# Sliding-window attention and soft-MoE slots: mask by a TensorE product, weight loads in quarter pieces in a fixed order

## The chip, the cores and the metric

The kernel runs on one core of one Trainium2 chip. The metric is the device time of one execution in microseconds, as the median of several runs; one further execution is profiled. PE is the matrix engine (TensorE), PEld its weight loads, DVE VectorE, ACT ScalarE, POOL GpSimd, SP the engine that issues the output transfers.

## The reference

Causal sliding-window attention (window 64) over q, k, v of 8 batches, 8 heads, 576 positions, 64 values per head; its output, as x of 4608 rows by 512, goes through a soft mixture of 8 experts with 4 slots each.

```python
scores = scale * np.matmul(q, k.transpose(0, 1, 3, 2))
rel = pos[:, None] - pos[None, :]
mask = (rel >= 0) & (rel < window)
scores = np.where(mask, scores, -1000000000.0)
attn = softmax(scores, -1)
x = (attn @ v) laid out as (B * S, H * D)

logits = x @ phi                                  # (4608, 32)
d = softmax(logits, 0); slot_input = d.T @ x      # 32 slots
slot_out[e] = np.maximum(slot_input[e] @ w1[e], 0.0) @ w2[e]   # e = 0..7
return softmax(logits, 1) @ slot_out
```

Inputs and output are 32-bit floats; w1[e] is 512 x 1024, w2[e] 1024 x 512.

## The kernel before

The attention runs over 16 units; a unit is one half (four heads) of one batch. Its q, k and v are loaded by three transfers issued on Pool's queue (`load_unit`, line 56), which also turn them into 16-bit floats, 288 KB each in SBUF; three buffers of each kind rotate. A weight tile, w1 or w2 of one expert, is one transfer of 1024 KB on the same queue (`load_w1`, `load_w2`, lines 70 and 74); the w2 of the last expert goes in two transfers into a buffer that held attention output. Eight w1 and seven w2 buffers mean that no other weight load waits for a buffer.

Work on unit u is cut into three steps j (eight windows of 64 queries in steps 0 and 1, one window per head pair in step 2). In each step the loop of lines 316 to 332 emits:

- `stage_t2(u, j)` (line 160): PE transposes of v (line 167) into a PSUM tile `tr`, and two copies on VectorE into `vw` (line 169);
- `stage_s(u, j)` (line 173): score matmuls (line 182) into the PSUM tile `sc`, the two halves x of the heads lying on partitions 0 to 63 and 64 to 127 and in two banks; Exp on ScalarE into `pm` (line 187); then the mask, two products on VectorE (line 191) with the 0/1 tile `mask0`;
- `stage_t1(u + 1, j)` (line 147): PE transposes of the next unit's q (j = 0), k (j = 1) or v (j = 2) (line 136) in two `tr` tiles, copied to SBUF by ScalarE for q and v (line 143), by VectorE for k (line 141);
- `stage_av` of the step before (line 198): the attention product (line 214) and the division on VectorE (lines 220 to 231); line 229 writes the last chunk of a unit;
- one piece of the MoE work of a finished batch (`stage_xt` to `stage_et`, lines 241 to 294), each with a `tr`-tagged PSUM tile.

`tr` has two PSUM buffers, `sc` two, `av` one. After unit 15 come the rest of the MoE work, `dinv` and `slot_inT` (lines 351 and 352), then the experts (`hp` line 362, `sop` line 382) and the output stage (`cp` line 398, `ob` lines 402 and 404, output transfers from SP).

The program is written with a tile framework. The order on each engine is not that of the source: a scheduler takes, among the instructions that it holds ready, the one of the highest priority (source order), and so a transfer that waits for no buffer can go ahead of one that does. `issue_loads` (line 303) hands it one unit's loads and one weight tile per unit:

```python
def issue_loads(u):
    if u + 2 < nu:
        load_unit(u + 2)
    for _ in range(1 if u >= 1 else 0):
        if w_order and len(w_order) > 3:
            f, e = w_order.pop(0)
            f(e)
```

Of the kernel before, what the change touches and what calls it, by code (L numbers as in the profile page):

```python
# [9 lines left out]
FP16 = mybir.dt.float16  # L10
AF = mybir.ActivationFunctionType
ALU = mybir.AluOpType
# [4 lines left out]
def kernel(  # L17
# [10 lines left out]
    nc = tc.nc  # L28

    B, H, S, Dh = q.shape  # L30
    D, NSLOT = moe_phi.shape
    E, _, F = moe_w1.shape
# [4 lines left out]
    NHD = D // 128  # L37
    NFC = F // 128
# [15 lines left out]
    loaded = {}  # L54
# [12 lines left out]

    w1_t, w2_t = {}, {}

    def load_w1(e):  # L70
        w1_t[e] = pw1.tile([128, NHD, F], FP16, name="w1s", tag="w1s")
        nc.gpsimd.dma_start(out=w1_t[e], in_=moe_w1[e].rearrange("(c p) f -> p c f", p=128))

    def load_w2(e):
        src = moe_w2[e].rearrange("(c p) d -> p c d", p=128)
        if e < E - 1:
            w2_t[e] = pw2.tile([128, NFC, D], FP16, name="w2s", tag="w2s")
            nc.gpsimd.dma_start(out=w2_t[e], in_=src)
        else:
            w2_t[e] = pxb.tile([128, NFC, D], FP16, name="w2l", tag="x_bp")  # L80
            for c in range(0, NFC, 4):
                nc.gpsimd.dma_start(out=w2_t[e][:, c:c + 4], in_=src[:, c:c + 4])

    load_unit(0)

# [2 lines left out]
    make_identity(nc, ident)  # L88
    ones = const.tile([128, 128], FP16, name="ones")
    nc.vector.memset(ones, 1.0)  # L90
    mask0 = const.tile([128, 64], FP16, name="mask0")
    nc.gpsimd.memset(mask0, 1.0)
    nc.gpsimd.affine_select(
        out=mask0, in_=mask0, compare_op=ALU.is_ge, fill=0.0,
        base=-1, pattern=[[-1, 64]], channel_multiplier=1,
    )
    nc.gpsimd.affine_select(
        out=mask0, in_=mask0, compare_op=ALU.is_ge, fill=0.0,
        base=64, pattern=[[1, 64]], channel_multiplier=-1,
    )  # L100
    kTs, vTs, vws, hTs = [], [], [], []
    for n in range(2):
        kt = const.tile([128, 2, 64 + S], FP16, name=f"kT{n}")
# [20 lines left out]
        hTs.append(ht)  # L124

    psum1 = ExitStack()
    ps = psum1.enter_context(tc.tile_pool(name="ps", bufs=2, space=bass.MemoryType.PSUM))


    def t1(src, dst, on_vector):  # L130

        for t0, n in ((0, 5), (5, 4)):
            tr = ps.tile([128, 8, 128], FP16, name="tr", tag="tr")
            for j in range(n):
                for x in range(2):
                    nc.tensor.transpose(tr[64 * x:64 * x + 64, j, :],  # L136
                                        src[:, x, 64 * (t0 + j):64 * (t0 + j) + 64], ident[:, :])
            o = dst.rearrange("p h (g t) -> p h g t", t=T)[:, :, :, t0:t0 + n]
            i = tr[:, 0:n, :].rearrange("p t (h g) -> p h g t", h=2)
            if on_vector:  # L140
                nc.vector.tensor_copy(out=o, in_=i)  # L141
            else:
                nc.scalar.copy(out=o, in_=i)  # L143

    state = {}

    def stage_t1(u, which):
        if which == 0:
            qT = pqt.tile([128, 2, S], FP16, name="qT", tag="qT")
            state[u] = dict(qT=qT, kT=kTs[u % 2], vT=vTs[u % 2], vw=vws[u % 2])  # L150
            t1(loaded[u][0], qT, False)
        elif which == 1:
            t1(loaded[u][1], state[u]["kT"][:, :, 64:64 + S], True)
        else:
            t1(loaded[u][2], state[u]["vT"][:, :, 64:64 + S], False)

    def steps(j):
        return range(4 * j, 4 * j + 4) if j < 2 else range(8, 9)
# [1 line left out]
    def stage_t2(u, j):  # L160
        st = state[u]
        wins = list(steps(j))
        n = len(wins)
        tr = ps.tile([128, 8, 128], FP16, name="tr", tag="tr")
        for h in range(2):
            for w, i in enumerate(wins):
                nc.tensor.transpose(tr[:, h * n + w, :], st["vT"][:, h, 64 * i:64 * i + 128], ident[:, :])  # L167
        for h in range(2):
            nc.vector.tensor_copy(  # L169
                out=st["vw"][:, wins[0]:wins[0] + n, h::2, 0:64],  # L170
                in_=tr[:, h * n:h * n + n, :].rearrange("p w (x d) -> p w x d", x=2))

    def stage_s(u, j):
        st = state[u]
        wins = list(steps(j))
        n = len(wins)
        sc = ps.tile([128, 2, 512], FP32, name="sc", tag="sc")
        for h in range(2):
            for w, i in enumerate(wins):
                for x in range(2):  # L180
                    o = 64 * (h * n + w)
                    nc.tensor.matmul(sc[:, x, o:o + 64],
                                     st["kT"][64 * x:64 * x + 64, h, 64 * i:64 * i + 128],
                                     st["qT"][64 * x:64 * x + 64, h, 64 * i:64 * i + 64],
                                     start=True, stop=True)
        pm = ppm.tile([128, 2, 8, 64], FP16, name="pm", tag="pm")
        nc.scalar.activation(pm[:, :, 0:2 * n, :],  # L187
                             sc[:, :, 0:128 * n].rearrange("p x (w q) -> p x w q", q=64),
                             AF.Exp, scale=scale)
        for x in range(2):  # L190
            nc.vector.tensor_tensor(  # L191
                out=pm[:, x, 0:2 * n, :], in0=pm[:, x, 0:2 * n, :],
                in1=mask0[:, :].unsqueeze(1).broadcast_to([128, 2 * n, 64]), op=ALU.mult)
        st["pm", j] = pm

    xbp = {}
# [1 line left out]
    def stage_av(u, j):  # L198
        b, half = units[u]
        st = state[u]  # L200
        bp, odd = divmod(b, 2)
        if bp not in xbp:
            xbp[bp] = pxb.tile([128, 9, D], FP16, name="x_bp", tag="x_bp")
        xb = xbp[bp]
        wins = list(steps(j))
        n = len(wins)
        pm = st["pm", j]
        av = ps.tile([128, 4, 256], FP32, name="av", tag="av", bufs=1)
        for x in range(2):
            for h in range(2):  # L210
                kk = 2 * x + h
                for w, i in enumerate(wins):
                    r0 = 64 * (i % 2) if j < 2 else 64 * odd
                    nc.tensor.matmul(av[r0:r0 + 64, kk, 65 * (w // 2):65 * (w // 2) + 65],  # L214
                                     pm[:, x, h * n + w, :], st["vw"][:, i, kk, 0:65],
                                     start=True, stop=True)
        rc = psm.tile([128, 4, 2], FP32, name="rc", tag="rc")
        if j < 2:
            avv = av[:, :, 0:130].rearrange("p k (c e) -> p k c e", e=65)
            nc.vector.reciprocal(rc[:, :, :], avv[:, :, :, 64])  # L220
            c0 = 4 * odd + 2 * j
            nc.vector.tensor_tensor(  # L222
                out=xb[:, c0:c0 + 2, 256 * half:256 * half + 256].rearrange("p c (k d) -> p k c d", d=64),
                in0=avv[:, :, :, 0:64],
                in1=rc[:, :, :].unsqueeze(3).broadcast_to([128, 4, 2, 64]), op=ALU.mult)
        else:
            r = slice(64 * odd, 64 * odd + 64)
            nc.vector.reciprocal(rc[r, :, 0], av[r, :, 64])
            nc.vector.tensor_tensor(  # L229
                out=xb[r, 8, 256 * half:256 * half + 256].rearrange("p (k d) -> p k d", d=64),  # L230
                in0=av[r, :, 0:64],
                in1=rc[r, :, 0].unsqueeze(2).broadcast_to([64, 4, 64]), op=ALU.mult)
# [62 lines left out]


    nu = len(units)
    w_order = []
    for e in range(E):
        w_order += [(load_w1, e), (load_w2, e)]  # L300
    w_at = {u: 1 for u in range(3, nu)}

    def issue_loads(u):
        if u + 2 < nu:
            load_unit(u + 2)
        for _ in range(1 if u >= 1 else 0):
            if w_order and len(w_order) > 3:
                f, e = w_order.pop(0)
                f(e)

    load_unit(1)
    todo = []
# [2 lines left out]
    pend = None  # L315
    for u in range(nu):
        issue_loads(u)
        for j in range(3):
            stage_t2(u, j)
            stage_s(u, j)  # L320
            if u + 1 < nu:
                stage_t1(u + 1, j)
            if pend is not None:
                stage_av(*pend)
                pu, pj = pend
                if pj == 2 and units[pu][1] == 1:
                    b = units[pu][0]
                    todo += [lambda b=b: stage_xt(b, 0), lambda b=b: stage_xt(b, 1), lambda b=b: stage_xt(b, 2),
                             lambda b=b: stage_logit(b), lambda b=b: stage_slot(b), lambda b=b: stage_et(b)]
            pend = (u, j)  # L330
            if todo:
                todo.pop(0)()
    while w_order:
        f, e = w_order.pop(0)
        f(e)
    stage_av(*pend)
    while todo:
        todo.pop(0)()
# [106 lines left out]
```

## Time and profile before

| | us |
|---|---|
| median of 3 runs (lowest, highest) | 244.25 (244.11, 244.54) |
| the profiled execution | 244.91 |
| its span, first to last instruction | 243.0 |
| PE busy | 168.3 (69%) |
| PEld busy | 121.0 (50%) |
| DVE busy | 147.1 (61%) |
| ACT busy | 100.9 (42%) |
| POOL busy | 51.7 (21%) |

Pool's loads, the software queue, move 30.97 MB as written to SBUF; the outputs, on a hardware queue, 9.44 MB. The busy shares are means over stages that differ: attention, experts, output. The page cuts the span into 40 slices with the busy share of each engine, the granted PE clock (PEclk) and the DMA rate; other views give the instructions in order of time, stretches with busy times, groups of like instructions with their mean duration, and the chain of work that ended last. Busy time of PE includes modelled ends of pipelined matmuls.

### The profile page before, as it was taken

Reading aid. Unit: us, or ns where it says so; the run is one execution under the profiler, and the core shown is the slowest. Engines: PE = TensorE matmul, PEld = TensorE weight load, DVE = VectorE, ACT = ScalarE, POOL = GpSimd, SP = SyncE. Lnnn points to the kernel's source line nnn. Section 1 sums busy time; section 2 is a strip of 40 time slices with the busy share of each in tenths; the row PEclk is TensorE's granted clock in tenths of the full one; section 3 lists DMA queues with packets and bytes.
Section 4 is the critical chain, followed back from the end, with each engine's and each line's share of the span. In section 5 each row is a group of like instructions: output and inputs, shape, how many; then the busy total and the mean of one; then the engine's idle time right before and its main releaser. Section 6 shows DMA issues by size and latency. Waiting matters only on the chain. (4 is left out here: it accounts for less than half of the span.)

```text
span 243.0 us, 6919 instructions
## 1 busy us (share of the span) xinstructions
PE 168.3 (69%) x3028; PEld 121.0 (50%) x3028; DVE 147.1 (61%) x420; ACT 100.9 (42%) x160; POOL 51.7 (21%) x77
## 2 busy tenths in 40 slices
PE   0687677878862858749388699777866899878000
PEld 0466566667651746538266577666655444321000
DVE  1258898898882663917457486998996212199100
ACT  2456547537540705325071437367340211199000
POOL 8953342222322123231122321002000000000000
PEclk9999999999996555965756657999996599965555
DMA  5999999999999999999999999006500000079996
GB/s 86 159 192 211 206 207 210 208 209 211 208 212 205 209 208 208 211 206 211 207 209 208 207 206 163 2 3 94 84 3 0 3 0 4 0 270 378 379 374 154
DMA packets 31069, 40.83 MB, mean 168 GB/s; under 512 B 1856, under 2 KB 22336, under 8 KB 31040
## 3 DMA queue, kind: packets, MB, share of 16 engines
q0 software_dynamic: 26144, 30.97, 74.8%
q1 hardware_dynamic: 4896, 9.44, 11.3%
q8 instruction: 23, 0.38, 0.6%
q14 instruction: 6, 0.05, 0.1%
HBM read 61.93 MB, written 9.44 MB: 294 GB/s over the span
## 5 line engine op out<-in xcount | busy, mean ns | idle before, releaser
L187 ACT ACTIVATE pm<-sc 128x1024 f16<-128x1024 f32 (+1 forms) x48 | 39.1, 814 | 25.0 <-issue 18.9
L191 DVE TENSOR_TENSOR pm<-pm,mask_98 128x512 f16<-128x512 f16 (+1 forms) x96 | 30.0, 352 | 1.6 <-ACT pm L187 1.1
L136 PE MATMUL tr<-ident,vn 128*64 128x128 f16 x288 | 17.3, 258 | 19.7 <-DMA vn<-in_v_dram 17.6
L143 ACT COPY qT<-tr 128x640 f16<-128x640 f16 (+1 forms) x32 | 23.4, 746 | 10.5 <-PE tr L136 10.4
L143 ACT COPY vT_112<-tr 128x640 f16<-128x640 f16 (+1 forms) x16 | 11.8, 739 | 32.3 <-PE tr L136 32.1
L214 PEld LDWEIGHTS <-pm 128*64 128x64 f16 x576 | 21.5, 126 | 5.8 <-DVE x_bp L229 2.2
L136 PEld LDWEIGHTS <-vn 128*64 128x64 f16 x288 | 12.7, 131 | 21.2 <-DMA vn<-in_v_dram 18.8
L143 ACT COPY vT_103<-tr 128x640 f16<-128x640 f16 (+1 forms) x16 | 11.7, 739 | 27.0 <-PE tr L136 25.5
L220 DVE RECIPROCAL rc<-av 128x8 f32<-128x8 f32 x32 | 6.4, 199 | 27.2 <-PE av L214 27.2
L222 DVE TENSOR_TENSOR x_bp<-av,rc 128x512 f16<-128x512 f32 x32 | 22.0, 686 | 0.4
L136 PE MATMUL tr<-ident,qn 128*64 128x128 f16 x288 | 17.1, 263 | 6.8 <-DMA qn<-in_q_dram 5.6
L169 DVE COPY vw_104<-tr 128x512 f16<-128x512 f16 (+1 forms) x48 | 14.9, 351 | 9.4 <-PE tr L167 9.4
L136 PE MATMUL tr<-ident,kn 128*64 128x128 f16 x288 | 15.6, 249 | 5.6 <-DMA kn<-in_k_dram 2.6
L61 POOL DMA_DIRECT2D vn<-in_v_dram x16 | 11.4, 715 | 33.0 <-DMA w2s<-in_moe_w_dram 8.4
L167 PE MATMUL tr<-ident,vT_112 128*128 128x128 f16 x144 | 14.7, 251 | 5.2 <-ACT vT_112 L143 2.6
L169 DVE COPY vw_113<-tr 128x512 f16<-128x512 f16 (+1 forms) x48 | 15.1, 349 | 4.9 <-PE tr L167 4.9
L167 PE MATMUL tr<-ident,vT_103 128*128 128x128 f16 x144 | 15.2, 250 | 3.7 <-ACT vT_103 L143 1.5
L249 PE MATMUL tr<-ident,x_bp 128*128 128x128 f16 x144 | 13.3, 240 | 5.5 <-DVE kT_111 L141 2.7
L136 PEld LDWEIGHTS <-qn 128*64 128x64 f16 x288 | 11.8, 132 | 10.1 <-DMA qn<-in_q_dram 5.6
L141 DVE COPY kT_102<-tr 128x640 f16<-128x640 f16 (+1 forms) x16 | 11.7, 768 | 7.6 <-PE tr L136 7.4
L61 POOL DMA_DIRECT2D kn<-in_k_dram x16 | 11.4, 714 | 21.1 <-PE tr L136 6.9
L214 PE MATMUL av<-vw_113,pm 128*64 128x65 f16 x288 | 14.3, 216 | 1.3 <-DVE x_bp L229 0.8
(78 smaller groups left out, 284.7 us busy)
## 6 DMA issues: line engine op xcount, KB each, us to landing
out_dram<-ob SPq DMA_DIRECT2D x18, 512.0 KB, 5.5
w1s<-in_moe_w_dram POOLq DMA_DIRECT2D x8, 1024.0 KB, 25.1
w2s<-in_moe_w_dram POOLq DMA_DIRECT2D x7, 1024.0 KB, 22.1
qn<-in_q_dram POOLq DMA_DIRECT2D x16, 288.0 KB, 17.4
kn<-in_k_dram POOLq DMA_DIRECT2D x16, 288.0 KB, 15.3
vn<-in_v_dram POOLq DMA_DIRECT2D x16, 288.0 KB, 16.3
w2l<-in_moe_w_dram POOLq DMA_DIRECT2D x2, 512.0 KB, 8.6
phi_sb<-in_moe_phi_dram POOLq DMA_DIRECT2D x1, 32.0 KB, 6.4
```

The costliest lines, as they stand in the source:

```text
L61: nc.gpsimd.dma_start(out=t, in_=src[b, 4 * half:4 * half + 4].rearrange("(x h) (g t) d -> (h g) x (t d)", x=2, h=2, t=T))
L136: nc.tensor.transpose(tr[64 * x:64 * x + 64, j, :], src[:, x, 64 * (t0 + j):64 * (t0 + j) + 64], ident[:, :])
L141: nc.vector.tensor_copy(out=o, in_=i)
L143: nc.scalar.copy(out=o, in_=i)
L167: nc.tensor.transpose(tr[:, h * n + w, :], st["vT"][:, h, 64 * i:64 * i + 128], ident[:, :])
L169: nc.vector.tensor_copy(out=st["vw"][:, wins[0]:wins[0] + n, h::2, 0:64], in_=tr[:, h * n:h * n + n, :].rearrange("p w (x d) -> p w x d", ...
L187: nc.scalar.activation(pm[:, :, 0:2 * n, :], sc[:, :, 0:128 * n].rearrange("p x (w q) -> p x w q", q=64), AF.Exp, scale=scale)
L191: nc.vector.tensor_tensor(out=pm[:, x, 0:2 * n, :], in0=pm[:, x, 0:2 * n, :], in1=mask0[:, :].unsqueeze(1).broadcast_to([128, 2 * n, 64]), ...
L214: nc.tensor.matmul(av[r0:r0 + 64, kk, 65 * (w // 2):65 * (w // 2) + 65], pm[:, x, h * n + w, :], st["vw"][:, i, kk, 0:65], start=True, sto ...
L220: nc.vector.reciprocal(rc[:, :, :], avv[:, :, :, 64])
L222: nc.vector.tensor_tensor(out=xb[:, c0:c0 + 2, 256 * half:256 * half + 256].rearrange("p c (k d) -> p k c d", d=64), in0=avv[:, :, :, 0:64 ...
L249: nc.tensor.transpose(tr[:, 4 * n + kk, :], xb[:, c, 128 * kk:128 * kk + 128], ident[:, :])
```

## The change

1. The 0/1 mask on VectorE is gone. A constant `hide` holds, for each query row of a 64-row half, 0 where a key is seen and -30000 where not; `rep` holds eight copies of a 64 x 64 identity per half. Per step, two matmuls (one per half x, 512 columns in steps 0 and 1, 128 in step 2) put the mask into `sc` ahead of the scores, and the scores are accumulated onto it.
2. Each w1 and w2 is loaded in two pieces of 512 KB. From unit 1 to unit 13 two pieces follow the unit's loads where u is odd and one where it is even, and the remaining twelve follow at unit 14. Pool's instructions from here on keep the order of the source (`manual_schedule`).
3. Both k copies of `t1` go to ScalarE, and the second of the two v copies to VectorE.
4. `stage_t2` orders its transposes so that one VectorE copy of up to 1024 elements replaces two of up to 512.

```diff
+    def load_w(e, n):
+        if n == 0:
+            w1_t[e] = pw1.tile([128, NHD, F], FP16, name="w1s", tag="w1s")
+        if n == 2:
+            if e < E - 1:
+                w2_t[e] = pw2.tile([128, NFC, D], FP16, name="w2s", tag="w2s")
+            else:
+                w2_t[e] = pxb.tile([128, NFC, D], FP16, name="w2l", tag="x_bp")
+        if n < 2:
+            c = slice(2 * n, 2 * n + 2)
+            nc.gpsimd.dma_start(out=w1_t[e][:, c], in_=moe_w1[e].rearrange("(c p) f -> p c f", p=128)[:, c])
         else:
+            c = slice(4 * n - 8, 4 * n - 4)
+            nc.gpsimd.dma_start(out=w2_t[e][:, c], in_=moe_w2[e].rearrange("(c p) d -> p c d", p=128)[:, c])
...
+    rep = const.tile([128, 8, 64], FP16, name="rep")
+    for h in range(2):
+        nc.gpsimd.tensor_copy(
+            out=rep[64 * h:64 * h + 64, :, :],
+            in_=ident[64 * h:64 * h + 64, 64 * h:64 * h + 64].unsqueeze(1).broadcast_to([64, 8, 64]))
+    hide = const.tile([128, 128], FP16, name="hide")
+    nc.gpsimd.memset(hide, 0.0)
+    for h in range(2):
+        m = hide[64 * h:64 * h + 64, :]
+        nc.gpsimd.affine_select(out=m, in_=m, compare_op=ALU.is_ge, fill=-30000.0,
+                                base=-1, pattern=[[1, 128]], channel_multiplier=-1)
+        nc.gpsimd.affine_select(out=m, in_=m, compare_op=ALU.is_ge, fill=-30000.0,
+                                base=64, pattern=[[-1, 128]], channel_multiplier=1)
...
     psum1 = ExitStack()
+    psum1.enter_context(tc.manual_schedule(engines={mybir.EngineType.Pool}))
...
-            t1(loaded[u][0], qT, False)
+            t1(loaded[u][0], qT, (nc.scalar, nc.scalar))
         elif which == 1:
-            t1(loaded[u][1], state[u]["kT"][:, :, 64:64 + S], True)
+            t1(loaded[u][1], state[u]["kT"][:, :, 64:64 + S], (nc.scalar, nc.scalar))
         else:
-            t1(loaded[u][2], state[u]["vT"][:, :, 64:64 + S], False)
+            t1(loaded[u][2], state[u]["vT"][:, :, 64:64 + S], (nc.scalar, nc.vector))
...
-        for h in range(2):
-            nc.vector.tensor_copy(
-                out=st["vw"][:, wins[0]:wins[0] + n, h::2, 0:64],
-                in_=tr[:, h * n:h * n + n, :].rearrange("p w (x d) -> p w x d", x=2))
+        nc.vector.tensor_copy(
+            out=st["vw"][:, wins[0]:wins[0] + n, :, 0:64],
+            in_=tr[:, 0:2 * n, :].rearrange("p (w h) (x d) -> p w (h x) d", h=2, x=2))
...
+        for x in range(2):
+            nc.tensor.matmul(sc[:, x, 0:128 * n], hide[64 * x:64 * x + 64, :],
+                             rep[64 * x:64 * x + 64, 0:2 * n, :], start=True, stop=False,
+                             skip_group_check=True)
...
-                                     start=True, stop=True)
+                                     start=False, stop=(h == 1 and w == n - 1), skip_group_check=True)
...
-        for x in range(2):
-            nc.vector.tensor_tensor(
-                out=pm[:, x, 0:2 * n, :], in0=pm[:, x, 0:2 * n, :],
-                in1=mask0[:, :].unsqueeze(1).broadcast_to([128, 2 * n, 64]), op=ALU.mult)
...
+    w_order = [(e, n) for e in range(E) for n in range(4)]
     def issue_loads(u):
         if u + 2 < nu:
             load_unit(u + 2)
+        if 1 <= u < nu - 2:
+            for _ in range(1 + u % 2):
+                load_w(*w_order.pop(0))
...
         issue_loads(u)
+        if u == nu - 2:
+            while w_order:
+                load_w(*w_order.pop(0))
```

## Rows read from the trace of the kernel before

**Rows 1.** The page's 40 slices of the span, 6.1 us each: DMA and GB/s.

```profile
DMA  5999999999999999999999999006500000079996
GB/s 86 159 192 211 206 207 210 208 209 211 208 212 205 209 208 208 211 206 211 207 209 208 207 206 163 2 3 94 84 3 0 3 0 4 0 270 378 379 374 154
```

**Rows 2.** Timeline, VectorE, line 229: start us, duration us, engine, line, operation.

```profile
23.67 0.41 DVE L229 TENSOR_TENSOR x_bp<-av,rc 64x256 f16<-64x256 f32 x1
...
68.16 0.41 DVE L229 TENSOR_TENSOR x_bp<-av,rc 64x256 f16<-64x256 f32 x1
...
127.10 0.41 DVE L229 TENSOR_TENSOR x_bp<-av,rc 64x256 f16<-64x256 f32 x1
...
140.27 0.43 DVE L229 TENSOR_TENSOR x_bp<-av,rc 64x256 f16<-64x256 f32 x1
...
151.14 0.43 DVE L229 TENSOR_TENSOR x_bp<-av,rc 64x256 f16<-64x256 f32 x1
...
178.98 0.43 DVE L229 TENSOR_TENSOR x_bp<-av,rc 64x256 f16<-64x256 f32 x1
...
185.62 0.43 DVE L229 TENSOR_TENSOR x_bp<-av,rc 64x256 f16<-64x256 f32 x1
```

**Rows 3.** Timeline, Pool's DMA issues, 61 to 70 us; in brackets the wait ahead.

```profile
61.29 0.90 POOL L78 DMA_DIRECT2D w2s<-in_moe_w_dram  x1 [4.00 <-DMA w1s<-in_moe_w_dram]
...
64.20 0.77 POOL L72 DMA_DIRECT2D w1s<-in_moe_w_dram  x1 [0.48 <-DMA qn<-in_q_dram]
69.45 0.70 POOL L61 DMA_DIRECT2D vn<-in_v_dram  x1 [4.48 <-PE tr L249]
```

**Rows 4.** Chain that ended last: start us, duration us, engine, tile, line, instructions.

```profile
189.66 1.68 PE hp L362 x13
...
208.38 2.84 PE sop L382 x13
```

**Rows 5.** Windows: length; PE, PEld, DVE, ACT, POOL busy us (instructions); clock, DMA, GB/s.

```profile
20.00:68.16 48.16, 37.79 (x911) 30.34 (x908) 41.78 (x121) 29.22 (x45) 15.14 (x20) 1.00 1.19 209
68.16:127.10 58.94, 39.16 (x696) 31.20 (x696) 32.42 (x92) 21.05 (x34) 14.88 (x20) 0.64 1.19 209
74.00:76.00 2.00, 0.00 (x0) 0.00 (x0) 0.24 (x2) 0.00 (x0) 0.00 (x0) 0.58 1.17 203
142.00:144.00 2.00, 1.99 (x29) 1.52 (x27) 1.54 (x5) 0.38 (x1) 0.00 (x0) 0.50 1.22 207
```

**Rows 6.** Timeline, PE, at the higher clock and after the starved wait.

```profile
19.34 0.41 PE L182 MATMUL sc<-qT,kT_111 64*128 64x64 f16 x16
...
22.02 0.47 PE L136 MATMUL tr<-ident,qn 128*64 128x128 f16 x10
...
22.55 0.32 PE L182 MATMUL sc<-qT,kT_111 64*128 64x64 f16 x10
...
77.76 0.74 PE L136 MATMUL tr<-ident,vn 128*64 128x128 f16 x10 [4.68 <-DMA vn<-in_v_dram]
```

**Rows 7.** Timeline, all engines, the start.

```profile
1.30 0.81 POOL L61 DMA_DIRECT2D qn<-in_q_dram  x1 [0.80 <-POOLq L429]
...
5.62 1.17 PE L136 MATMUL tr<-ident,qn 128*64 128x128 f16 x18 [5.62 <-DMA qn<-in_q_dram]
...
7.02 0.72 POOL L61 DMA_DIRECT2D qn<-in_q_dram  x1
```

**Rows 8.** The page's groups: line, operation, count, busy us, mean ns of one, idle before.

```profile
L191 DVE TENSOR_TENSOR pm<-pm,mask_98 128x512 f16<-128x512 f16 (+1 forms) x96 | 30.0, 352 | 1.6 <-ACT pm L187 1.1
...
L143 ACT COPY qT<-tr 128x640 f16<-128x640 f16 (+1 forms) x32 | 23.4, 746 | 10.5 <-PE tr L136 10.4
...
L141 DVE COPY kT_102<-tr 128x640 f16<-128x640 f16 (+1 forms) x16 | 11.7, 768 | 7.6 <-PE tr L136 7.4
```

**Rows 9.** Groups by line with each shape apart: PSUM copies on VectorE.

```profile
L169 DVE COPY vw_113<-tr 128x512 f16<-128x512 f16 x32 | 12.2, 416 | 4.9 <-PE tr L167 4.9
...
L251 DVE COPY xT<-tr 128x1024 f16<-128x1024 f16 x16 | 11.0, 690 | 2.5 <-PE tr L249 2.4
```

More of the change, by code (lines that the diff above doesn't have):

```diff
@@ L68 @@
     w1_t, w2_t = {}, {}
[L70 to L78, printed above, removed]
-        else:
-            w2_t[e] = pxb.tile([128, NFC, D], FP16, name="w2l", tag="x_bp")
-            for c in range(0, NFC, 4):
-                nc.gpsimd.dma_start(out=w2_t[e][:, c:c + 4], in_=src[:, c:c + 4])
+    def load_w(e, n):
[9 more added lines that the diff above has]
+            nc.gpsimd.dma_start(out=w1_t[e][:, c], in_=moe_w1[e].rearrange("(c p) f -> p c f", p=128)[:, c])
+        else:
+            c = slice(4 * n - 8, 4 * n - 4)
+            nc.gpsimd.dma_start(out=w2_t[e][:, c], in_=moe_w2[e].rearrange("(c p) d -> p c d", p=128)[:, c])
     load_unit(0)
@@ L90 @@
     nc.vector.memset(ones, 1.0)
[L91 to L100, printed above, removed]
+    rep = const.tile([128, 8, 64], FP16, name="rep")
[11 more added lines that the diff above has]
+                                base=64, pattern=[[-1, 128]], channel_multiplier=1)
     kTs, vTs, vws, hTs = [], [], [], []
@@ L126, with t1 @@
     psum1 = ExitStack()
+    psum1.enter_context(tc.manual_schedule(engines={mybir.EngineType.Pool}))
     ps = psum1.enter_context(tc.tile_pool(name="ps", bufs=2, space=bass.MemoryType.PSUM))
-    def t1(src, dst, on_vector):
-        for t0, n in ((0, 5), (5, 4)):
+    def t1(src, dst, engines):
+        for (t0, n), eng in zip(((0, 5), (5, 4)), engines):
             tr = ps.tile([128, 8, 128], FP16, name="tr", tag="tr")
@@ L139, in t1 @@
             i = tr[:, 0:n, :].rearrange("p t (h g) -> p h g t", h=2)
-            if on_vector:
+            if eng is nc.vector:
                 nc.vector.tensor_copy(out=o, in_=i)
@@ L164, in stage_t2 @@
         tr = ps.tile([128, 8, 128], FP16, name="tr", tag="tr")
-        for h in range(2):
-            for w, i in enumerate(wins):
-                nc.tensor.transpose(tr[:, h * n + w, :], st["vT"][:, h, 64 * i:64 * i + 128], ident[:, :])
-        for h in range(2):
-            nc.vector.tensor_copy(
-                out=st["vw"][:, wins[0]:wins[0] + n, h::2, 0:64],
-                in_=tr[:, h * n:h * n + n, :].rearrange("p w (x d) -> p w x d", x=2))
+        for w, i in enumerate(wins):
+            for h in range(2):
+                nc.tensor.transpose(tr[:, 2 * w + h, :], st["vT"][:, h, 64 * i:64 * i + 128], ident[:, :])
+        nc.vector.tensor_copy(
+            out=st["vw"][:, wins[0]:wins[0] + n, :, 0:64],
+            in_=tr[:, 0:2 * n, :].rearrange("p (w h) (x d) -> p w (h x) d", h=2, x=2))
     def stage_s(u, j):
@@ L214, in stage_av @@
                     nc.tensor.matmul(av[r0:r0 + 64, kk, 65 * (w // 2):65 * (w // 2) + 65],
-                                     pm[:, x, h * n + w, :], st["vw"][:, i, kk, 0:65],
+                                     pm[:, x, h * n + w, :], st["vw"][:, i, 2 * h + x, 0:65],
                                      start=True, stop=True)
@@ L297 @@
     nu = len(units)
[L298 to L301, printed above, removed]
+    w_order = [(e, n) for e in range(E) for n in range(4)]
     def issue_loads(u):
@@ L305, in issue_loads @@
             load_unit(u + 2)
[L306 to L309, printed above, removed]
+        if 1 <= u < nu - 2:
+            for _ in range(1 + u % 2):
+                load_w(*w_order.pop(0))
     load_unit(1)
@@ L332 @@
                 todo.pop(0)()
-    while w_order:
-        f, e = w_order.pop(0)
-        f(e)
     stage_av(*pend)
```

## The prediction, made before the changed kernel ran

> **What bounds the kernel now.** I read the 40 slices first. The DMA row stands at 9 from the second slice to the 25th and GB/s is flat near 208 [rows 1]: about 31 MB land between 3 and 152 us. That looks like a kernel bound by its loads for 150 us, but the kernel runs on for 90 us behind them, so the question is which loads come when. The write of the last chunk of each unit marks the 16 units [rows 2]: unit 0 at 23.7 and unit 5 at 68.2, so (68.16 - 23.67) / 5 = 8.90 us each; unit 9 at 127.1, so 14.7 us each for four; from 151.1 to 179.0 three more at 9.28 us; unit 15 after 6.6 us, because it has no next unit to transpose.
>
> The queue explains the slow ones. Between 61 and 70 us Pool issues a whole w2, a whole w1 and only then the v that the next unit waits for [rows 3]. One unit's q, k, v are 3 x 288 KB = 0.885 MB of fp16, one weight tile is 1.049 MB; two weight tiles and a unit are 2.98 MB, at 208 GB/s 14.3 us, which is the 14.4 to 14.7 us seen. So in this stretch the attention starves behind weights that nobody needs before 189.66 us [rows 4], and once the weights are in, a backlog of four units remains to be computed with the DMA idle. In the fast stretch VectorE is the bound: 41.78 of 48.16 us busy, against 37.79 for PE and 29.22 for ScalarE; in the starved one it is busy 32.42 of 58.94 [rows 5]. Starving costs twice: a transpose waits 4.68 us for v [rows 6], the granted clock goes from 1.00 to 0.58 in 74 to 76 us, and the stretch has a mean of 0.64 [rows 5]; 1.00 is the level of 2.4 GHz, 0.50 that of 1.2.
>
> **The change, part by part.** *The load order.* Pool now issues in program order: units 0 to 2 without weights, then each unit followed by one or two quarter pieces (0.524 MB, 2.52 us), 20 pieces by v of unit 15, and 12 behind it. v of unit 15 is preceded by 14.16 + 10.49 MB = 24.65 MB, 118.5 us at 208 GB/s. The first transposes wait until 5.62 us for data [rows 7], the stream starts some 3 us in, so v of unit 15 lands at about 122 us; the last weight piece 12 x 2.52 us later, about 152. Before, it had to share with nearly all weights. The bound that loads put on the attention: the last v is transposed about 5 us before its previous unit ends, so unit 14 can't end before 127, i.e. 7.3 us per unit from a unit 0 at 24.7. Waiting buffers don't add to this: a v load waits for the transposes of three units before, and has two units' time (over 15 us) to land; behind it on Pool stand only weight pieces and the next q, k, v, which have the same time. Fifteen more DMA issues cost Pool about 0.8 us each, hidden, as Pool is mostly waiting. If that cover were gone, it would be 12 us spread over 150 us of loads.
>
> The pieces of the last expert land at about 152 us. Its w2 is used in the last stretch of sop, from 208.38 - 189.66 = 18.7 us after the expert stage begins [rows 4], its w1 a product earlier, so nothing waits there if that stage begins after some 136.
>
> *VectorE.* Removed: the mask products, 30.0 us over 16 units, 1.88 us per unit; the two k copies of 0.77 each, 1.54 per unit [rows 8]. Added: the second half of v at a k copy's price, 0.75. The two vw copies of 0.416 become one of 1024 elements, priced by xT at 0.690 [rows 9]: about -0.25 per unit with the small ones. From 41.78 / 48.16 x 8.90 = 7.72 us per unit to 4.8.
>
> *ScalarE.* k copies added at qT's price, 2 x 0.746 = 1.49 [rows 8]; half of v gone, -0.74. From 29.22 / 48.16 x 8.90 = 5.40 to 6.15 us per unit.
>
> *TensorE.* Six mask matmuls per unit, four of 512 columns, two of 128, each on half of the rows. No row shows 512 columns on half of the rows. Bounds: one after the other at the pace of sop, 2.84 / 13 = 0.218 us [rows 4], gives 4 x 0.218 + 2 x 0.055 = 0.98 us per unit; in pairs, as the score matmuls on the two halves go, half of that, 0.49: sixteen scores take 0.41 us and ten 0.32 [rows 6], so six more cost 0.09, 15 ns each, where 64 columns one by one at 2.4 GHz are 27. I take 0.5, as the scores use the same halves and banks. PE: 37.79 / 48.16 x 8.90 = 6.98, then 7.5 us per unit, at most 8.0. At the lower clock twice as much.
>
> *The two tr buffers.* Twelve tiles per unit pass through them: six of t1 (fill 0.47 [rows 6], a tenth between, evacuation 0.75 [rows 8]: about 1.3 each), two large and one small of t2 (1.4, 1.4, 0.5), three of the MoE part (about 2.9 together). Sum 14.0, over two buffers 7.0 us per unit if no evacuation ever waits for its engine. That is a floor; before, the same sum stood under 8.9.
>
> *The start.* Pool has two copies (512 elements on 64 partitions each), a memset and four selects ahead of unit 1's loads, in place of a memset and two selects. No row shows such a copy. Everything that Pool does from the first q to unit 1's q, six loads' and memsets' worth and more, takes 7.02 - 1.30 = 5.7 us [rows 7]; a third of that, 2 us, is my upper bound (an estimate), and 0 the lower, since unit 1's loads may still be early enough. I take 1.
>
> *New pace.* Nothing in the new kernel is as full as VectorE was. Busy times per unit: PE 7.5, tr buffers 7.0, loads 7.3, ScalarE 6.15, VectorE 4.8. The fast stretch ran its fullest engine at 0.87. By that the pace would be 7.5 / 0.87 = 8.6; but PE's busy time counts drains that overlap, and in 142 to 144 us PE was busy 1.99 of 2 [rows 5]. At 0.91 it is 8.2, which I take. Bounds: 7.3 (loads) and 8.0 / 0.85 = 9.4.
>
> *Sum.* Unit 0 ends at 23.7 + 1 = 24.7; unit 14 at 24.7 + 14 x 8.2 = 139.5; unit 15 6.6 later, 146.1; from there to the first hp 189.66 - 185.62 = 4.0 [rows 2, 4], 150.1; expert and output stages unchanged, 243.0 - 189.66 = 53.3: span 203.4. The profiled run had 244.91 for a span of 243.0, so 205.3; it lies 0.66 above the median 244.25, so 204.7. **I predict 205.** Each 0.1 us of pace is 1.4 us.
>
> **The rivals.** *A, the loads become the pace* (7.3 to 7.7): for it, each engine's sum is below 7.6; against it, several resources lie so close that each will wait for the others. 24.7 + 14 x 7.4 + 6.6 + 4.0 + 53.3 + 1.9 - 0.7 = 193.
>
> *B, TensorE, the tr buffers and ScalarE wait for each other* (8.8 to 10): both t1 evacuations of q and of k stand behind an Exp on one engine, holding both tr buffers, where k's were on the other before. At 9.4: 221. Against it: at that pace ScalarE would be busy only 6.15 of 9.4 us.
>
> *C, quarter pieces cost the queue.* A lone load pays more than its bytes: the first q, issued at 1.30, is used at 5.62 us [rows 7], 4.3 us later, of which 1.4 is its bytes at 208 GB/s and 2.9 is not. If each DMA kept that to itself, ten more of them ahead of v of unit 15 put 29 us on it: 151, and the end at 151 + 5 + 6.6 + 4 + 53.3 + 1.2 = 221. Against it: the rate is near 208 in all slices from the fourth to the 24th, those of the last ones included, in which q, k and v of 288 KB make up most of the queue [rows 1]. The Trainium skill, DMA: Bandwidth & Descriptors, section Anatomy of one DMA, gives a fixed 2.0 us per DMA beside its bytes, and so speaks against small pieces; by it the ten would cost 20 us and the end would be 212. This trace does not bear out that the fixed part adds up.
>
> *D, the order is not what starves* (or isn't kept): the starved stretch stays, and only the three backlog units gain about 1 us each: 240 to 244.
>
> *E, slower: the clock stays low.* At the lower clock a unit took 151.14 - 140.27 = 10.9 us with data at hand and PE nearly always busy [rows 2, 5]; with 1.0 to 1.9 us of mask products on top, 11.9 to 12.8. If k of the 14 units run so, unit 15 ends at 146.1 + 4.2 k: above 185.6 from k = 10 on; with all 14 the time is 263. Against it: in this trace the clock fell after an idle PE of over 4 us, and stayed at 1.00 in 48 us at 0.785 busy [rows 5], and the new order leaves each load some 5 to 15 us early. The Trainium skill, TensorE: Matmul & The Clock Gate, section Part 4: PE-mode transpose, says that transposes do not count as work for the clock; by that a stage made mostly of transposes would stay low. The fast stretch here, mostly transposes by time, ran at 1.00, so the trace does not agree.
>
> **How the numbers follow.** Forecast (pace 7.7 to 8.8, 198 to 214) 0.54; A 0.13 (189 to 198); B 0.15 (214 to 229); C 0.05; D 0.05, a fifth of it within 0.2%, which is about what a measurement of this kernel can tell from no change; E 0.08. The range 193 to 224 takes in the forecast, C and some two thirds of A and B, about 0.79. Faster 0.91, the same 0.01, slower 0.08.
>
> **What would show it.** In the slices: DMA at 9 to about 152 us, but PEclk at 9 through the whole attention. Chunk writes of j = 2 evenly 8.2 us apart, none over 10. No wait of a transpose for q, k or v over 2 us after the first unit. First hp near 150. Per unit: VectorE near 4.8 busy, ScalarE near 6.2, PE near 7.5; mask matmuls in pairs, 0.21 us a pair. Wrong if the gaps exceed 9.4 with loads early (B), if transposes wait for v (C, D), or if PEclk shows 5 in the attention while PE is full (E). If the pace is 7.4 and the transposes wait for loads by a little, A.

## The result, and the profile after

| | us | ratio to the kernel before, 95% interval |
|---|---|---|
| kernel before, median of 4 | 244.39 | |
| changed kernel, median of 4 | 207.08 | 0.846 (0.841 to 0.850) |
| changed kernel, profiled execution | 206.54, span 204.8 | |

The ratio leaves out slow executions, here one of the four of the changed kernel (210.77 us). The forecast was 205, with a range from 193 to 224. The 40 slices of the changed kernel, 5.1 us each, answer to [rows 1]; PEclk is the granted clock in tenths:

```profile
PE   0899989999998999999999989989769998793000
...
PEclk9999999999999999999999999999987999755555
DMA  4899999999999999999999999999999200599995
GB/s 72 107 147 191 208 209 207 207 210 208 209 207 205 208 209 207 207 210 207 206 206 209 209 208 206 210 208 210 210 208 172 34 3 0 217 379 378 379 342 148
```

The same 31 MB stream in at the same 208 GB/s. The queue is full until about 156 us and empty by 162. Before, it was full until about 150 us, and the last tile (w2 of the last expert, issued at 164.71 us) came by itself in the 28th and 29th slice, 164 to 176 us; the prediction's "31 MB by 152" leaves that tile out. What moved is everything behind it: the output burst begins in the 35th slice of 5.1 us (174 us) where it began in the 36th of 6.1 us (213 us). And the clock stays up through the whole attention. The writes of the last chunk of a unit, on VectorE (start us, duration us), answer to [rows 2]; units 0, 5, 6, 14 and 15 of 16:

```profile
20.76 0.42 DVE L235 TENSOR_TENSOR x_bp<-av,rc 64x256 f16<-64x256 f32 x1
...
63.88 0.42 DVE L235 TENSOR_TENSOR x_bp<-av,rc 64x256 f16<-64x256 f32 x1
71.43 0.43 DVE L235 TENSOR_TENSOR x_bp<-av,rc 64x256 f16<-64x256 f32 x1
...
141.08 0.43 DVE L235 TENSOR_TENSOR x_bp<-av,rc 64x256 f16<-64x256 f32 x1
148.00 0.43 DVE L235 TENSOR_TENSOR x_bp<-av,rc 64x256 f16<-64x256 f32 x1
```

The pace, the mean gap between these writes, is (141.08 - 20.76) / 14 = 8.59 us. The single gaps run from 7.5 to 9.9, mostly in a repeating pattern of four (7.55, 9.22, 8.11, 9.93), and none is near the 14.7 of before. The stretch from 21 to 141 us (length; PE, PEld, DVE, ACT, POOL busy us; clock, DMA share, GB/s) answers to [rows 5], and three waits of the whole run (who waited for whom: us in total, times, longest) to [rows 6]:

```profile
21.00:141.00 120.00, 111.39 (x2477) 85.54 (x2475) 78.28 (x175) 83.51 (x128) 46.34 (x65) 1.00 1.20 208
```

```profile
ACT pm L197 <- PE sc L192: 19.6, 28, 1.2
...
PE tr L143 <- DMA qn<-in_q_dram: 5.7, 2, 5.5
...
PE tr L143 <- DMA vn<-in_v_dram: 0.4, 1, 0.4
```

After the first load of the run (5.5 us) no transpose waits more than 0.4 us for data. TensorE is busy 0.93 of the stretch, VectorE 0.65 (0.87 in the fast stretch of before), ScalarE 0.70. New is what the first line names: Exp on ScalarE now waits for the scores, 28 times. ScalarE's idle time ahead of Exp as such is not new; before it was 25.0 us in all, as the page's row shows (last number: idle before it):

```profile
L187 ACT ACTIVATE pm<-sc 128x1024 f16<-128x1024 f32 (+1 forms) x48 | 39.1, 814 | 25.0 <-issue 18.9
```

### The profile page after: what moved, and what is told of

The parts are those of the page before. It is cut to its first block, busy times and chain, and to the rows that moved or that the text cites. A ratio compares the mean times of both kernels' runs of the same rounds, so it can differ in the third digit from the quotient of the medians.

```text
span 204.8 us, 7004 instructions
## 1 busy us (share of the span) xinstructions
PE 165.1 (81%) x3124; PEld 112.8 (55%) x3124; DVE 109.0 (53%) x260; ACT 113.0 (55%) x176; POOL 63.3 (31%) x96
## 4 chain that ended last, share of the span: by engine, by line
PE 52%; ACT 24%; issue 5%; DMA 4%; POOL 3%; DVE 2%; ACTq 0%; POOLq 0%
PE tr L174 10%; ACT pm L197 9%; PE sop L384 8%; PE tr L143 6%; PE tr L255 5%; PE sc L192 5%; DMA vn<-in_v_dram 4%; ACT qT L150 4%; PE av L220 4%; PE cp L400 3%; PE pa L284 3%; ACT ob L404 3%; PE hp L364 3%; PE sc L185 3%; ACT kT_115 L150 2%
## 5 line engine op out<-in xcount | busy, mean ns | idle before, releaser
L197 ACT ACTIVATE pm<-sc 128x1024 f16<-128x1024 f32 (+1 forms) x48 | 39.2, 817 | 19.6 <-PE sc L192 19.6
L185 PE MATMUL sc<-rep,hide 64*128 64x512 f16 (+1 forms) x96 | 24.8, 342 | 0.0
L257 DVE COPY xT<-tr 128x1024 f16<-128x1024 f16 (+1 forms) x20 | 12.8, 638 | 12.8 <-PE tr L255 12.8
L81 POOL DMA_DIRECT2D w1s<-in_moe_w_dram x16 | 11.4, 712 | 16.8 <-DMA vn<-in_v_dram 5.2
L175 DVE COPY vw_117<-tr 128x1024 f16<-128x1024 f16 (+1 forms) x24 | 13.3, 555 | 5.4 <-PE tr L174 5.2
L61 POOL DMA_DIRECT2D qn<-in_q_dram x16 | 11.5, 719 | 13.1 <-PE av L220 4.2
L175 DVE COPY vw_126<-tr 128x1024 f16<-128x1024 f16 (+1 forms) x24 | 13.2, 551 | 4.0 <-PE tr L174 3.0
L84 POOL DMA_DIRECT2D w2s<-in_moe_w_dram x14 | 10.6, 754 | 14.5 <-DMA w1s<-in_moe_w_dram 7.0
L192 PE MATMUL sc<-qT,kT_115 64*128 64x64 f16 x288 | 13.8, 197 | 0.0
L174 PE MATMUL tr<-ident,vT_116 128*128 128x128 f16 x144 | 13.1, 227 | 0.7 <-DVE rc L226 0.4
L255 PEld LDWEIGHTS <-x_bp 128*128 128x128 f16 x144 | 9.5, 97 | 7.0 <-issue 6.1
L406 DVE TENSOR_SCALAR ob<-cp,crcp 128x512 f32<-128x512 f32 x18 | 12.6, 746 | 0.9 <-PE cp L400 0.8
## 6 DMA issues: line engine op xcount, KB each, us to landing
w2s<-in_moe_w_dram POOLq DMA_DIRECT2D x14, 512.0 KB, 14.7
```

What stands on the lines that cost most here:

```text
L61: nc.gpsimd.dma_start(out=t, in_=src[b, 4 * half:4 * half + 4].rearrange("(x h) (g t) d -> (h g) x (t d)", x=2, h=2, t=T))
L174: nc.tensor.transpose(tr[:, 2 * w + h, :], st["vT"][:, h, 64 * i:64 * i + 128], ident[:, :])
L175: nc.vector.tensor_copy(out=st["vw"][:, wins[0]:wins[0] + n, :, 0:64], in_=tr[:, 0:2 * n, :].rearrange("p (w h) (x d) -> p w (h x) d", h=2 ...
L185: nc.tensor.matmul(sc[:, x, 0:128 * n], hide[64 * x:64 * x + 64, :], rep[64 * x:64 * x + 64, 0:2 * n, :], start=True, stop=False, skip_gro ...
L192: nc.tensor.matmul(sc[:, x, o:o + 64], st["kT"][64 * x:64 * x + 64, h, 64 * i:64 * i + 128], st["qT"][64 * x:64 * x + 64, h, 64 * i:64 * i ...
L197: nc.scalar.activation(pm[:, :, 0:2 * n, :], sc[:, :, 0:128 * n].rearrange("p x (w q) -> p x w q", q=64), AF.Exp, scale=scale)
```

## The experiments

Each time is the median of four executions; the ratio is to the kernel before on the same chip. "Pace" is the time from the last chunk of unit 0 to that of unit 14, over 14. The runs were taken on several chips, so a difference of two runs is best read from the ratios.

| kernel | us | ratio (95% interval) | pace, us |
|---|---|---|---|
| changed kernel | 207.08 | 0.846 (0.841 to 0.850) | 8.59 |
| before + load order | 217.31 | 0.889 (0.883 to 0.894) | 9.14 |
| changed - load order | 234.56 | 0.959 (0.953 to 0.965) | uneven |
| changed, no mask at all | 201.33 | 0.821 (0.816 to 0.826) | 8.22 |
| changed, mask on VectorE | 202.16 | 0.827 (0.822 to 0.832) | 8.22 |
| changed, k copies on VectorE | 205.92 | 0.838 (0.833 to 0.843) | 8.53 |
| changed, whole weight tiles | 207.07 | 0.843 (0.839 to 0.847) | 8.60 |
| changed, one expert's weights | 207.16 | 0.844 (0.839 to 0.849) | 8.59 |
| changed, mask product twice | 214.01 | 0.871 (0.866 to 0.876) | 8.99 |
| mask on VectorE, MoE tiles in score buffers | 200.35 | 0.816 (0.812 to 0.820) | 8.08 |
| changed, MoE tiles in score buffers | 205.29 | 0.835 (0.832 to 0.839) | 8.33 |
| changed, mask and k copies on VectorE | 213.97 | 0.870 (0.863 to 0.876) | 8.96 |
| MoE tiles in score buffers, mask on VectorE, v copies on ScalarE | 201.51 | 0.825 (0.817 to 0.833) | 8.15 |

**The load order alone.** The kernel before with the loads of the changed one:

```diff
+    psum1.enter_context(tc.manual_schedule(engines={mybir.EngineType.Pool}))
...
-    def load_w1(e):
...
+    def load_w(e, n):
...
+    w_order = [(e, n) for e in range(E) for n in range(4)]
...
+        if 1 <= u < nu - 2:
+            for _ in range(1 + u % 2):
+                load_w(*w_order.pop(0))
...
```

> The kernel before with the new load order alone (quarter pieces, source order on Pool; mask, copies and transposes as before). Theory 1, the starved stretch was the loss: every unit then runs at the pace of the old fast stretch, 8.9 us, bound by VectorE; 23.7 + 14 x 8.9 + 6.6 + 4.0 + 53.3 + 1.2 = 213 us, granted clock 1.00 through the attention. Theory 2, the gain came from the lighter VectorE: 230 to 240 us.

Measured 217.31. The clock in its slices, and its stretch from 21 to 141 us:

```profile
PEclk9999979999999999999799999999655999855555
```

```profile
21.00:141.00 120.00, 97.07 (x2263) 78.69 (x2264) 104.72 (x296) 69.51 (x109) 45.29 (x63) 0.97 1.18 200
```

The order alone gives 27 of the 37 us. All 14 gaps lie between 8.6 and 10; the fullest engine is VectorE with 104.72 of 120. Theory 1 stands; its 213 were 4 short, as the pace is 9.14 and not 8.9, and the clock was 0.97 and not 1.00.

**All but the load order.** The changed kernel with the old `load_w1`, `load_w2` and `issue_loads`, and without `manual_schedule`:

```diff
-    psum1.enter_context(tc.manual_schedule(engines={mybir.EngineType.Pool}))
...
+        for _ in range(1 if u >= 1 else 0):
+            if w_order and len(w_order) > 3:
+                f, e = w_order.pop(0)
+                f(e)
...
```

> The changed kernel with the old loads (whole weight tiles, one per unit, order left to the scheduler); mask product and copies as changed. Theory 1: the units starve as before, gaps of over 14 us between the last chunks of the units in the middle, only the backlog at the end is computed faster; 232 to 242 us, and the clock falls to 0.5 there. Theory 2: 207 to 214 us.

Measured 234.56, theory 1. The clock again, and three of its transposes between 73 and 125 us (in brackets the wait ahead):

```profile
PEclk9999999999999657967859875799999799955555
```

```profile
77.77 0.74 PE L140 MATMUL tr<-ident,kn 128*64 128x128 f16 x10 [3.44 <-DMA kn<-in_k_dram]
...
100.31 0.47 PE L140 MATMUL tr<-ident,qn 128*64 128x128 f16 x10 [2.39 <-DMA qn<-in_q_dram]
...
114.91 0.74 PE L140 MATMUL tr<-ident,qn 128*64 128x128 f16 x10 [3.84 <-DMA qn<-in_q_dram]
```

Starving comes back, and the low clock with it. So of the 37.3 us, 27.3 are the order's without the rest and 10.0 the rest's without the order; here they happen to add up. "The order" stands for the places of the pieces and the order of the source on Pool together; no run separates the two.

**No mask, and the mask on VectorE.** Both drop the mask matmuls; the second brings the two products on `pm` back.

```diff
-        for x in range(2):
-            nc.tensor.matmul(sc[:, x, 0:128 * n], hide[64 * x:64 * x + 64, :],
-                             rep[64 * x:64 * x + 64, 0:2 * n, :], start=True, stop=False, ...)
...
-                                     start=False, stop=(h == 1 and w == n - 1), ...)
+                                     start=True, stop=True)
...  (the second kernel alone:)
+        for x in range(2):
+            nc.vector.tensor_tensor(out=pm[:, x, 0:2 * n, :], in0=pm[:, x, 0:2 * n, :],
+                in1=mask0[:, :].unsqueeze(1).broadcast_to([128, 2 * n, 64]), op=ALU.mult)
```

> The changed kernel without the mask matmuls; the scores start their own accumulation, and no mask is applied at all (part of the computation is left out). Theory P, TensorE's own stream sets the pace of 8.59 us: it falls by what the mask matmuls cost there, 0.5 (pairs side by side) to 1.0 us (one after the other) per unit, 193 to 200 us. Theory R, the two tr buffers and the queue of Exp and copies on ScalarE set it: the pace stays within 0.15 us of 8.59, 205 to 208 us.

> The changed kernel with the mask back on VectorE (two products on pm), all else as changed. Theory P: TensorE's 7.0 us and VectorE's 5.6 + 1.9 = 7.5 us per unit allow a pace of 8.0 to 8.3, 198 to 203 us. Theory R or a longer chain from Exp over the product to the attention product: pace 8.6 to 9, 207 to 213 us.

Measured 201.33 and 202.16, both at a pace of 8.22. The second is theory P's case; the first falls between the two theories, as the pace moved by 0.37, more than R's 0.15 and less than P's 0.5. The stretch from 21 to 141 us, first without a mask:

```profile
21.00:141.00 120.00, 104.42 (x2506) 85.80 (x2506) 81.78 (x186) 84.74 (x131) 46.10 (x64) 1.00 1.20 208
```

and with the mask on VectorE:

```profile
21.00:141.00 120.00, 103.10 (x2486) 84.28 (x2481) 105.29 (x276) 84.35 (x132) 45.52 (x64) 0.99 1.19 208
```

Without the matmuls TensorE has 104.42 / 120 x 8.22 = 7.15 us of work per unit, with them 111.39 / 120 x 8.59 = 7.97: they cost 0.82 of its busy time and 0.37 of pace. On VectorE the mask costs (105.29 - 81.78) / 120 x 8.22 = 1.61 us of busy time per unit and nothing of the pace: once the k copies are gone from it, VectorE has room for it (0.88 busy). So this part of the change costs 5 us, and undoing it alone beats both kernels.

**Where the product hurts: the mask twice.** A second pair of the same matmuls into the same scores.

```diff
-        for x in range(2):
-            nc.tensor.matmul(sc[:, x, 0:128 * n], hide[64 * x:64 * x + 64, :],
-                             rep[64 * x:64 * x + 64, 0:2 * n, :], start=True, stop=False,
...
+        for r in range(2):
+            for x in range(2):
+                nc.tensor.matmul(sc[:, x, 0:128 * n], hide[64 * x:64 * x + 64, :],
+                                 rep[64 * x:64 * x + 64, 0:2 * n, :], start=(r == 0), stop=False,
...
```

> The changed kernel with the mask product put into the scores twice (the same mask added once more; the result is the same). Taking it away changed the pace from 8.59 to 8.22 and TensorE's busy time by 0.8 us per unit. If the product lies on the chain from the free score buffer to Exp, the second one costs at least as much again: pace 8.95 to 9.1, 212 to 214. If TensorE's busy time itself is the bound, 0.8 more: 9.4, 218. If the cost is one of order alone (the wait, not the length): 207 to 209.

Measured 214.01, pace 8.99, the first case: none, one and two products give 8.22, 8.59 and 8.99. The stretch from 21 to 141 us of the kernel with two, and the wait of Exp for scores over the whole run in that kernel and then in the one with none:

```profile
21.00:141.00 120.00, 109.66 (x2440) 80.78 (x2439) 75.16 (x169) 78.67 (x123) 46.16 (x64) 1.00 1.19 207
```

```profile
ACT pm L198 <- PE sc L193: 28.3, 29, 1.5
```

```profile
ACT pm L193 <- PE sc L188: 1.2, 3, 0.5
```

TensorE's busy share went down with the second product, from 0.928 to 0.914, and per unit its busy time rose by 0.24 us where the pace rose by 0.40. So its busy time alone does not give the pace. The wait of Exp grows: 1.2, 19.6 and 28.3 us with none, one and two products. The chain of the changed kernel (start us, duration us, from 91 us on) passes through that place:

```profile
91.47 0.55 PE tr L174 x8
92.02 0.15 PE sc L192
...
92.25 1.02 ACT pm L197
93.28 0.65 ACT kT_115 L150
...
93.97 0.78 PE pa L284 x25
```

Transposes, scores, Exp, the copy that stands behind Exp on ScalarE, and then the next user of the `tr` buffer that this copy frees. One reading is that mask matmuls in front of the scores delay an Exp, and with it the copies that give the `tr` buffers back. No run shows this path, and two numbers speak against taking Exp's wait as its measure. The first is Exp's wait from 25 to 135 us with two products, and then in the changed kernel with its MoE tiles in the score buffers (a run told below, pace 8.33):

```profile
ACT pm L198 <- PE sc L193: 22.2, 22, 1.5
...
ACT pm L197 <- PE sc L192: 24.8, 31, 2.1
```

Exp waits longer there, and the pace is the faster one. The second is ScalarE's whole idle time in the stretch: 120 - 84.74 = 35.3 us without a mask and 120 - 83.51 = 36.5 with it, so most of the wait moved from the copies to Exp. Nor is TensorE excluded as part of the bound: it stands idle 1.07, 0.62 and 0.78 us per unit with none, one and two products. What is shown is the price, about 0.4 us of pace for each pair.

**The k copies back on VectorE.**

```diff
-            t1(loaded[u][1], state[u]["kT"][:, :, 64:64 + S], (nc.scalar, nc.scalar))
+            t1(loaded[u][1], state[u]["kT"][:, :, 64:64 + S], (nc.vector, nc.vector))
```

> The changed kernel with both k copies back on VectorE (ScalarE 6.0 to 4.5 us per unit, VectorE 5.6 to 7.1). Theory B, the copies that stand behind Exp on ScalarE hold the tr buffers and set the pace: it falls below 8.3 us, under 203 us. Theory M, the wait of Exp for mask and scores on TensorE sets it: within 0.15 of 8.59, 205 to 209 us. If VectorE's queue takes the place of ScalarE's: above 8.8, over 210.

Measured 205.92, pace 8.53. This is theory M's case, and theory B in its simple form falls: taking two copies from behind Exp moves the pace by 0.06. With the mask on TensorE it hardly matters which of the two engines copies k. With the mask on VectorE it does:

> The changed kernel with the mask and both k copies on VectorE, so that of the change the load order, the split of v and the joint vw copy remain. VectorE's work per unit: 7.2 + 1.5 = 8.7 us; if a full VectorE is the bound again, pace 8.9 to 9.2 and 211 to 217 us, near the order alone (9.14, 217.3). If the joint vw copy and the split of v had brought most of the gain: 8.2 to 8.6, 202 to 207 us.

Measured 213.97, pace 8.96, the first case. Its stretch from 21 to 141 us has VectorE at 0.93, and the clock at 1.00:

```profile
21.00:141.00 120.00, 96.10 (x2292) 78.95 (x2291) 111.41 (x276) 62.24 (x97) 45.66 (x64) 1.00 1.19 207
```

So the order of the gains is, from 217.3 (load order alone): the joint vw copy and the split of v bring 3 us, the k copies on ScalarE 12 more (202.2), and the mask on TensorE takes 5 back (207.1). By the ratios the three are 5, 10 and 5. The parts are not independent: the k copies bring all of that with the mask on VectorE and nothing with it on TensorE.

**Whole weight tiles, and the weights of one expert alone.** The first loads each tile whole at the place of its first piece (`if n == 1: return`, `c = slice(0, 4)`, and likewise for w2). The second leaves out the weights of all experts but the first:

```diff
     def load_w(e, n):
+        if e:
+            w1_t[e], w2_t[e] = w1_t[0], w2_t.get(0)
+            return
```

> The changed kernel with each weight tile in one whole load at the place of its first quarter piece; order otherwise the same. If each DMA kept a fixed cost to itself (rival C), sixteen fewer loads would show as a shorter stream by up to 2.9 us each. If the fixed part is covered, 206 to 208 us, DMA slices and the end of the stream within 1 us. If the pieces' size guards q, k, v from waiting behind a whole tile: transposes wait for loads, over 209.

> The changed kernel with the weights of expert 0 alone loaded and used for all experts (the other experts' weights are left out): from unit 4 on the queue carries q, k, v alone. Theory L, the full queue sets the pace: it falls towards 7.3 us, 190 to 194 us. Theory M: the pace stays within 0.15 of 8.59 and the time at 205 to 208.

Measured 207.07 and 207.16. DMA and GB/s of the second, where the queue is half empty from the 12th slice on:

```profile
DMA  4899999999985688768868700000000000699995
GB/s 69 110 139 195 208 211 207 205 208 206 207 143 82 108 115 118 97 86 113 105 86 111 113 3 5 3 0 5 3 3 0 0 3 0 225 377 379 379 340 145
```

Same pace, same time: with the new order the loads are off the path, and the queue's load doesn't slow the engines either. Theory L and rival A are out. And quarter pieces neither cost nor gain: with half as many weight loads the stream ends in the same slice (172, then 33 GB/s; in the changed kernel 172, then 34). It is the place in the queue that counts.

**The tr buffers.** The four PSUM tiles of the MoE part (`tr` of `stage_xt`, `lt`, `pa` and `te`) are moved to the score buffers, in the kernel with the mask on VectorE and in the changed one:

```diff
-        tr = ps.tile([128, 8, 128], FP16, name="tr", tag="tr")
+        tr = ps.tile([128, 8, 128], FP16, name="tr", tag="sc")
...
```

> The changed kernel with the mask on VectorE (as in e4_mask_on_vector, pace 8.22, 202.2 us), and the four PSUM tiles of the MoE part taken from the two score buffers in place of the two tr buffers. Theory R, the round through the two tr buffers sets the pace of 8.22: its sum falls from 14.0 to 11.1 us of buffer time per unit, the pace to 7.4 to 8.0, 191 to 199 us. If VectorE (7.2 of 8.22 busy) is the bound: within 0.15 of 8.22, 200 to 204 us. If the MoE tiles now hold up the scores: above 8.4, over 204 us.

> The changed kernel with the four PSUM tiles of the MoE part in the score buffers, mask on TensorE as changed. Theory R+M, the chain runs through the tr buffers and the mask products in turn: pace 7.9 to 8.4, 197 to 204 us. Theory M alone: within 0.15 of 8.59, 205 to 209 us. If the score buffers become scarce (mask, scores and Exp hold one for about 2 us already): above 8.75, over 209 us.

Measured 200.35 (pace 8.08) and 205.29 (8.33; this pace is in the range of R+M, the time in that of M alone). A fifth less work through the `tr` buffers, by the prediction's sum, brings 0.14 and 0.26 of pace: the buffers take part, but they don't set it alone, and the 7.4 to 8.0 of theory R is missed. 200.35 is the best kernel here. Its 8.08 is still the case named for a VectorE that is the bound, and VectorE is busy 104.22 of 120:

```profile
21.00:141.00 120.00, 104.81 (x2515) 85.37 (x2510) 104.22 (x280) 87.11 (x132) 45.41 (x63) 0.99 1.19 208
```

So the last run took work off it and gave it to ScalarE:

```diff
-            t1(loaded[u][2], state[u]["vT"][:, :, 64:64 + S], (nc.scalar, nc.vector))
+            t1(loaded[u][2], state[u]["vT"][:, :, 64:64 + S], (nc.scalar, nc.scalar))
```

> The kernel of e9_moe_in_sc (mask on VectorE, MoE tiles in the score buffers; pace 8.08, 200.4 us) with the second half of v copied by ScalarE as well. Per unit VectorE goes from 7.0 to 6.3 us, ScalarE from 5.9 to 6.6, TensorE stays at 7.1. Theory V, VectorE (0.87 busy) is the bound of 8.08: pace 7.5 to 7.9, 193 to 198 us. Theory Q, no engine alone but the copies that stand in line on ScalarE, each with transposes ahead of it: pace 8.1 to 8.5, 200.5 to 206 us.

Measured 201.51, pace 8.15. The stretch from 21 to 141 us:

```profile
21.00:141.00 120.00, 104.71 (x2510) 84.72 (x2509) 95.65 (x264) 96.47 (x146) 46.26 (x64) 0.98 1.19 208
```

No engine is over 0.88, and the pace didn't fall. That is theory Q's range, and VectorE alone is not the bound. Since the run moved work from VectorE to ScalarE at once, it does not show what a lighter ScalarE would do. What sets 8.1 stays open: past the start no transpose waits over 2 us for a load, and the chains show a round of transposes, copy and buffer return, but no run lengthened or shortened that round by itself.

## Why the prediction was right, point by point

The forecast's mechanism held: a queue that carried weights ahead of what the next unit waits for, and an attention that no longer starves once the order is mended. The total is 2 us off, but by terms that cancel (unit 0 is 3.9 us short of its sum, the 14 units 5.5 over), so that part of the closeness is luck:

| term | predicted | measured |
|---|---|---|
| unit 0 ends | 24.7 | 20.76 |
| 14 units at the pace | 14 x 8.2 = 114.8 | 14 x 8.59 = 120.3 |
| unit 15 | 6.6 | 6.92 |
| to the first hp | 4.0 | 3.85 |
| experts and output | 53.3 | 52.95 |
| span | 203.4 | 204.8 |

- **Unit 0** ended 4 us earlier than summed. I carried over 23.7 from before and added 1 for Pool's longer start. That start is 2.2 us longer, a little over my upper bound (unit 1's q is issued at 9.25 us instead of 7.02), but its transposes wait only 0.2 us for it. Before, the write at 23.67 stood behind the next unit's copies and mask products on VectorE; the relief that I costed for every later unit I forgot for the first. That this is all of it is not shown: unit 0 ended at 23.50 with the load order alone, but at 21.36 with mask and k copies on VectorE again, and at 23.68 with the mask product twice.
- **The pace** is the mis-sized term, and in it the mask products. I had 0.49 and 0.98 us per unit as ends and took 0.5, for pairs that go side by side; 0.82 was measured, within those ends. The pairs do go side by side when they are issued together, as the first of these PE lines of the changed kernel shows (start us, duration us, count): two last 0.39 us, as long as one. (My sign of 0.21 us a pair was too short.)

```profile
63.56 0.39 PE L185 MATMUL sc<-rep,hide 64*128 64x512 f16 x2
...
69.37 0.39 PE L185 MATMUL sc<-rep,hide 64*128 64x512 f16 x1
```

  The Trainium skill, TensorEngine Tiling (Array Packing), section Tiling Modes, says that different tiles can execute matmuls in parallel. The first row agrees. But the scheduler put other work between the halves of most pairs: between 21 and 141 us 8 pairs of 512 columns stand together and 40 halves alone. This fits a cost nearer to two singles than to a pair; no run kept all pairs together to test it.
- **What the products do to the pace** was reasoned on TensorE's busy share (7.5 at 0.91). The runs show that this rule does not hold: the share fell when the product was doubled. A pair of products costs 0.37 to 0.40 us of pace; by which path is not shown. That 0.91 came near (0.928) was not earned by the argument for it.
- **VectorE** fell to 78.28 / 120 x 8.59 = 5.60 us per unit, not 4.8: I took away the whole time of each group, but instructions that follow each other on VectorE overlap in the rows, so that taking a group out frees less than its own row says. In the kernel before, this copy ends at 14.11 us, 0.09 after the mask product behind it has started:

```profile
13.35 0.76 DVE L169 COPY vw_104<-tr 128x512 f16<-128x512 f16 x2 [2.69 <-PE tr L167]
14.02 0.75 DVE L191 TENSOR_TENSOR pm<-pm,mask_98 128x512 f16<-128x512 f16 x2
```

  By the busy time of the stretches the mask is worth 1.61 us per unit and not 1.88, and the k copies 111.41 / 120 x 8.96 - 105.29 / 120 x 8.22 = 1.11 and not 1.54. **ScalarE** came out at 5.98 (6.15).
- **The loads** ran at full rate to about 156 us and ended by 162 instead of 152, hidden either way. By the code 18 pieces, not 20, are issued ahead of v of unit 15 and 14 behind it. It was issued at 113.07 us and transposed at 139.33 without a wait; no transpose after the first load waited over 0.4 us.
- **The signs.** The first hp came at 151.85 us (near 150). The gaps were not even: three of the 14 (9.94, 9.94 and 9.93) passed the 9.4 that was to be B's sign, though their mean did not.
- **Rivals.** A fell with the one-expert run. B did not come, at 8.59 and not 9.4: fewer tiles in the `tr` buffers bring 0.26 of pace, so they take part, but k's copies behind Exp, its main premise, are worth 0.06. C fell with the whole tiles: sixteen loads more or less change neither the time nor the end of the stream. The Trainium skill's fixed 2.0 us per DMA (DMA: Bandwidth & Descriptors, Anatomy of one DMA) is not an addend in a full queue here. D fell with the load order alone (217.31); its case of an order that isn't kept is what the run with the old order shows, at 234.6 rather than 240. E did not occur: the clock was 1.00 from 21 to 141 us, also without the mask matmuls (1.00 and 0.99), where transposes are about two thirds of TensorE's busy time. In that stretch it was 0.97 or more in every run with the new order (0.97 with the order alone) and fell to one half only in those with the old one, behind waits for loads (3.44, 2.39 and 3.84 us in the run with the old order). The Trainium skill's sentence that transposes don't count as work for the clock (TensorE: Matmul & The Clock Gate, Part 4: PE-mode transpose) doesn't show here; as other matmuls stand among the transposes, no run tests it by itself.

What the prediction didn't ask is whether each part of the change pays. It costed the mask on TensorE at 0.5 us per unit and never set that against leaving the mask on a VectorE relieved of the k copies, for which the same table gave 4.8 + 1.9 = 6.7 us of 8.2.

## What to carry to other kernels

A DMA row at 9 says that the queue is full, not that the kernel is bound by it: look at which transfer the stalled engine waits for, and what was issued ahead of it. Put the order of loads down by first use, and weights that are needed last behind everything else. When work is moved off a full engine, price what is left there afterwards before moving more: the second move here, the mask, went from an engine with room for it to one where it cost 0.37 us of every unit.

## What was not expected of the hardware

- Two matmuls of 512 columns on the two halves of the rows, into two banks, took 0.39 us together, as long as one alone (0.37 to 0.39).
- A queue at 208 GB/s against one at about 110 made no difference to the pace of the engines (8.59 and 8.59): no cost of the traffic itself was seen.
- Doubling the mask products lowered TensorE's busy share (0.928 to 0.914) while the time rose by 7 us: a busy share of over 0.9 did not by itself show the bound.
